# Eight 64x32 array tiles in place of four 64x64 ones, in a convolution and two-layer kernel on one Trainium2 core

## The chip, the core and the metric

The kernel runs on one core of one Trainium2 chip. The metric is the time of one execution on the device, in microseconds (us). Two executions of the kernel before took 680.85 and 681.15 us, median 681.0 us. The profile is of one further execution. In it, PE is TensorE's matmul row and PEld its weight-load row; each matmul instruction is preceded by one weight load of its own. DVE is VectorE, ACT is ScalarE, POOL is GpSimd and SP is the queue of SyncE.

## The reference

The input x has 8 sequences of 4096 tokens with 192 features. A causal convolution over 7 tokens, with one softmaxed 7-tap filter for each of 8 heads of 24 features, gives y. Then every token goes through two dense layers with a leaky ReLU between them.

```python
w = softmax(weight)                       # 8 heads x 7 taps
y[b, s, h, :] = sum_k w[h, k] * x_pad[b, s + k, h, :]
h = y @ w_in                              # 192 -> 2048
g = maximum(0.01 * h, h)
out = g @ w_out                           # 2048 -> 192, for 32768 tokens
```

The two products are 25.8 billion multiply-adds. The output has 32768 rows of 192 float32 values.

## The kernel before

The sequences are taken in pairs (index e, 0 or 1), 512 tokens of each at a time: a *block*, of which there are 32. The first two blocks are split into halves of 256 tokens, so the list `groups` has four half groups (indices 0 to 3) and 30 whole groups (indices 4 to 33). The order in which each engine gets its instructions is the order in which they are written; nothing reorders them.

**First product** (`mm1`, line 507). Features stand on partitions, 64 of sequence 0 on partitions 0 to 63 and 64 of sequence 1 on partitions 64 to 127, in three chunks c. For one u (128 of the 2048 hidden units, 16 values of u for a group), `mm1` takes the three chunks, in each the two sequences e, and in each the hidden units in slices of M: one weight load and one matmul for each. With M = 64 there are four matmuls for each c, which use four tiles of the array, 64 rows by 64 columns each: e picks the upper or lower 64 rows of the array, the slice m picks the columns and so the partitions of the output. Each sequence has its own PSUM bank. A group has 16 x 3 x 4 = 192 such matmuls, each over 512 columns (tokens). The leaky ReLU runs on ACT (line 515), from PSUM to the tile `g`, once for each u.

**Second product.** Up to and including the first whole group, `mm2_row_slot` (line 525) makes out with tokens on partitions. From the second whole group on, that is from index 5 (`i > NSW`, NSW = 4), `mm2_slot` (line 588) makes it transposed: 64 output features on partitions, for sequence 0 on the lower and sequence 1 on the upper 64, tokens as columns. One slot is one group of 128 hidden units, in two row halves rt of 64, each for both sequences e: four matmuls in four 64x64 tiles. The two row halves write to two different accumulators of the three. A group has 3 x 16 slots, so again 192 matmuls over 512 columns.

The loop at the end alternates, for each of 8 steps j: `mm1` for two u, then 5, 5, 6, 5, 5, 6, 8 and 8 slots of the second product, of the group before. Between them it issues VectorE's convolution of the next group. DVE also transposes the finished accumulators (line 610), from where they are stored.

Each matmul starts only after its weight load; the weight load of a tile's next matmul may run beside the current matmul. A matmul that has to wait for a buffer carries a semaphore wait; the others carry none. Of PE's 12442 matmuls, 672 signal a semaphore.

Near the start of the kernel the first convolution is done on PE instead (line 259): matmuls over 256 columns in 64x64 tiles with a weight load each.

The diff touches a constant, `w_out_of`, `mm2_slot` and the call of `mm1`.

Of the kernel before, what the change touches and what calls it, by code (L numbers as in the profile page):

```python
# [15 lines left out]
def kernel(  # L16
# [19 lines left out]
    CH = 64  # L36
# [15 lines left out]
    SKEW += [(1, 5), (0, 6), (1, 6)]  # L52
    CUTS = {1: (0, 6), 3: (6, 11), 5: (11, 14)}
    GB = 32
    NR = D // (2 * GB)

    const_pool = ctx.enter_context(tc.tile_pool(name="const", bufs=1))
# [177 lines left out]
    def y_of(grp, c):  # L235
        blk, t0, T = grp
        if blk not in yt:
            yt[blk] = yt_pool.tile([128, NCH, ST], BF16, name="yt")
        return yt[blk][:, c, t0 : t0 + T]
# [59 lines left out]
    for sign, off in ((1, 0), (-1, GRP - 1)):  # L299
        nc.gpsimd.affine_select(  # L300
            out=sel[:, :, 0, :], in_=sel[:, :, 0, :], compare_op=mybir.AluOpType.is_ge,
# [45 lines left out]
    w_out = const_pool.tile([128, NFC, D], BF16)  # L347
    for h in range(2):
        cs = slice(h * NFC // (2 * RUN), (h + 1) * NFC // (2 * RUN))
        nc.gpsimd.dma_start(  # L350
            out=w_out.rearrange("p (c i) d -> p c i d", i=RUN)[:, cs],
# [6 lines left out]
    def warm(n, cols=HT, to=wa[:, 0]):  # L358
# [10 lines left out]
        out=nmax, in_=w9[:, 0:K], axis=mybir.AxisListType.X,  # L369
# [3 lines left out]
        out=w9[:, 0:K], in_=w9[:, 0:K], func=mybir.ActivationFunctionType.Exp,  # L373
# [18 lines left out]
    def select(out, parts):  # L392
# [17 lines left out]
        out=taps, in_=wps_hm[..., None].to_broadcast([128, NCH, 2, K + 1, 2])  # L410
# [5 lines left out]
    def diag_wide(c, p):  # L416
# [22 lines left out]
        out=rsum, in0=wml[:, :, K:], scalar=1e-9, in1=taps[:, :, 0, K:, 0],  # L439
# [14 lines left out]
    def act_scale(out, in_, scale):  # L454
# [11 lines left out]
        out=y_of(groups[0], 0), in0=hi[:, :HT], scalar=rsum[:, 0, :], in1=low,  # L466
# [12 lines left out]
    g, po, acc2, osb, seal = {}, {}, {}, {}, None  # L479
    NSW = 2 * NHALF  # L480
# [7 lines left out]
    def mm1(grp, u, M):  # L488
        blk, t0, T = grp
        y = yt[blk]  # L490
        nf = ST // T
        ph = psum_h.tile([128, 2, ST], FP32, name="ph", tag="ph")
        chunks = range(NCH)


        wide = not (blk or t0 or u)
        order = [(i, c) for i in range(nf) for c in chunks]
        if wide:
            order = [(i, c) for c in chunks for i in range(nf)]
        for i, c in order:  # L500
            if wide and (i, c) == (0, 2):
                transpose_first(1)
            f = nf * u + i
            for e in range(2):
                ps = slice(e * CH, (e + 1) * CH)
                for m in range(0, 128, M):
                    nc.tensor.matmul(  # L507
                        out=ph[m : m + M, e, i * T : (i + 1) * T],
                        lhsT=w_in_of(f, e, c, m, m + M),
                        rhs=y[ps, c, t0 : t0 + T],  # L510
                        start=(c == chunks[0] and not (wide and i)),
                        stop=(c == chunks[-1]),
                        skip_group_check=wide,
                    )
        act = nc.scalar.activation(  # L515
            out=g[blk][:, nf * u : nf * (u + 1), :, t0 : t0 + T],
            in_=ph.rearrange("p e (i t) -> p i e t", i=nf),
            func=mybir.ActivationFunctionType.Prelu, alpha=0.01,
        )
        return act  # L520
# [41 lines left out]
            seal = evac_o(2 * p - 1)  # L562
        sync(seal, ins, "between the rounds")

    def w_out_of(ps, fc, r):
        return w_out[ps, fc, r::NR]

    def mm2_slot(q):

        nonlocal seal
        gi, fc = divmod(q, NR * NFC)
        rnd, fc = divmod(fc, NFC)
        first, last = fc == 0, fc == NFC - 1
        if first:
            for r in ((1, 0), (2,), ())[rnd]:
                acc2[gi, r] = psum_o.tile([128, ST], FP32, name="acc2", tag="po")  # L580
        for rt in range(2):
            r = (rnd + rt) % NR
            fresh = (rnd, rt) in ((0, 0), (0, 1), (1, 1))
            done = (rnd, rt) in ((1, 0), (2, 0), (2, 1))
            b, t0, T = groups[gi]
            ps = slice(rt * CH, (rt + 1) * CH)
            for e in range(2):
                ins = nc.tensor.matmul(  # L588
                    out=acc2[gi, r][e * CH : (e + 1) * CH, 0:T],
                    lhsT=w_out_of(ps, fc, r),  # L590
                    rhs=g[b][ps, fc, e, t0 : t0 + T],
                    start=first and fresh,
                    stop=last and done,
                )
                if first and not fresh:
                    sync(ins, seal, "the other row tile has left this bank")
        if last and rnd < 2:
            seal = nc.scalar.copy(out=junk, in_=junk)  # L598
            sync(seal, ins, "between the rounds")
        if last and rnd > 0:  # L600
            for r in ((), (1,), (0, 2))[rnd]:
                evac_t(gi, r)

    def evac_t(gi, r):
# [3 lines left out]
        if (gi, 0) not in osb:  # L608
            osb[gi, 0] = o_pool.tile([128, ST // GB, GB, NR], FP32, name="o_t")
        nc.vector.transpose(  # L610
            out=osb[gi, 0][:, 0 : T // GB, :, r],
            in_=acc2.pop((gi, r))[:, 0:T].rearrange("p (j k) -> p j k", k=GB),
        )
# [4 lines left out]
        for e in range(2):  # L618
            rows = out_rows[2 * rp + e, st * ST + t0 : st * ST + t0 + T, :].rearrange(
                "(j k) d -> k j d", k=GB  # L620
            )
            parts = 2 if gi == len(groups) // 2 else 1
            for h, q in product(range(2), range(parts)):
                p = (2 * e + h) * GB
                js = slice(q * T // GB // parts, (q + 1) * T // GB // parts)
                nc.sync.dma_start(
                    out=rows[:, js, h * NR * GB : (h + 1) * NR * GB],
                    in_=t[p : p + GB, js].rearrange("p j k r -> p j (k r)"),
# [41 lines left out]
    for i, grp in enumerate(groups):  # L670
        blk, t0, T = grp
        steps = T // 64
        if t0 == 0:
            g[blk] = g_pool.tile([128, NFC, 2, ST], BF16, name="g", tag="g")
        quota = plan.get(i, [16] * 4 if T == HT else [5, 5, 6, 5, 5, 6, 8, 8])

        if i == 0:
            ahead = []
        else:
            ahead = conv_jobs(groups[i + 1]) if i + 1 < len(groups) else []  # L680
        per = -(-len(ahead) // steps)
        for j in range(steps):
            early = between.get((i, j), (0, 0))
            for u in range(2 * j, 2 * j + 2):
                mm2_slots(i, early[u % 2])
                mm1(grp, u, 128 if i <= NSW else CH)
                if i == 0 and u == 0:
                    evac_first(1, nc.vector.tensor_copy, nc.vector.tensor_copy)
                    spread_up(0, slice(2, 3), far)
                    conv_1 = conv_jobs(groups[1], (1,))  # L690
                    run([conv_1[:3]])
                    spread_down(1)
                    spread_up(1, slice(0, 1), near)
                    spread_up(1, slice(2, 3))
                    run([conv_1[3:5]])
                    spread_up(1, slice(0, 1), far)
                    run([conv_1[5:]])
                    pe_0, evac_0 = pe_conv_jobs(groups[1], 0)
                    pe_2, evac_2 = pe_conv_jobs(groups[1], 2, cross=True)
                if i == 0 and u in CUTS:  # L700
                    cut = slice(*CUTS[u])
                    run(pe_0[cut], pe_2[cut])
                if i == 0 and u == 5:
                    evac_0(nc.vector.tensor_scalar_mul)
                    evac_2(nc.vector.tensor_scalar_mul, nc.vector.tensor_scalar_mul)
                if i == 0 and u == 6:
                    transpose_first(2)
                    evac_first(2, nc.vector.tensor_copy, nc.vector.tensor_copy)
            jobs = ahead[per * j : per * (j + 1)]
            if T == ST:  # L710


                jobs = ahead[len(ahead) * j // steps : len(ahead) * (j + 1) // steps]
                for job in jobs:
                    job()
                jobs = []
            mm2_slots(i, quota[j] - sum(early))
            if i == 1 and j == 1:
                load_x(3, transpose_x(2))
            for job in jobs:  # L720
                job()
            if i == 0 and j == 3:
                transpose_half(3)

            last_half = t0 + T == ST
            if i == NSW and j == steps - 1:
                evac_o(LAST - 1)
                slot = NSW * NR * NFC
            if j == steps // 4 and last_half and blk > 0:
                load_x(blk + 3)  # L730
            if j == steps // 2 and last_half and blk > 0:
                transpose_x(blk + 2)
# [35 lines left out]
```

## Time and profile before

| | |
|---|---|
| time, median of 2 runs | 681.0 us (680.85 to 681.15) |
| span of the profiled execution | 679.2 us |
| PE busy | 674.9 us, 12442 matmuls |
| PEld busy | 446.3 us, 12442 weight loads |
| DVE busy | 481.2 us |
| ACT busy | 517.6 us |
| granted TensorE clock | 1.000 throughout |
| DMA | 53.27 MB, of them 1.59 MB instructions in 97 packets |

The span is the time from the first to the last instruction in one execution. It leaves 1.8 us of the 681.0 us outside. The busy time of PE counts overlapping matmuls once; the mean duration of one matmul (376 ns for 512 columns) is longer than its share of the time, as several run at once. A line number is that of the listing above.

### The profile page before, as it was taken

To read this page: it belongs to the slowest core of one execution; us is meant where nothing else is said; L and a number is where in the kernel's file an instruction comes from. 1 tells how busy PE (TensorE), PEld (TensorE's weight loads), DVE (VectorE), ACT (ScalarE), POOL (GpSimd) and SP (SyncE) were. 2 spreads that over 40 slices of the span, in tenths; PEclk is the share of its full clock that TensorE was granted. 3 is DMA by queue.
4 is the path that set the end of the run, shared out by engine and by line. 5 is a ranking of instruction groups with operands and counts; after the bars stand their busy time and mean duration, and the time that the engine had idled before them with its cause. 6 is when DMAs were issued, how large, how long until landed. Compare 5 with 4: busy or idle time off the path is not lost.

```text
span 679.2 us, 27092 instructions
## 1 busy us (share of the span) xinstructions
PE 674.9 (99%) x12442; PEld 446.3 (66%) x12442; DVE 481.2 (71%) x816; ACT 517.6 (76%) x601; POOL 147.4 (22%) x208
## 2 busy tenths in 40 slices
PE   9999999999999999999999999999999999999998
PEld 6997666666666666666666666666666666666667
DVE  7989477866768766778667687667786676876612
ACT  7899877777787777777777777778777777777781
POOL 8455221122211222211222112222022220000000
PEclk9999999999999999999999999999999999999999
DMA  9999755655737656556556566567365573321123
GB/s 149 99 119 104 52 85 83 84 64 67 96 74 93 76 54 86 84 85 86 66 63 92 80 92 78 56 83 94 73 87 69 60 96 71 72 56 33 34 49 94
DMA packets 213970, 53.27 MB, mean 78 GB/s; under 512 B 209312, under 2 KB 213536, under 8 KB 213856
## 3 DMA queue, kind: packets, MB, share of 16 engines
q0 software_dynamic: 98832, 13.97, 30.3%
q1 hardware_dynamic: 115008, 37.57, 28.0%
q8 instruction: 97, 1.59, 0.9%
q14 instruction: 17, 0.14, 0.1%
q10 hardware_dynamic: 16, 0.00, 0.0%
HBM read 28.31 MB, written 25.17 MB: 79 GB/s over the span
## 4 chain that ended last, share of the span: by engine, by line
PE 98%; DVE 1%; ACT 0%; issue 0%; ACTq 0%
PE ph L507 49%; PE acc L588 44%; PE po L525 5%; PE acc L259 0%; DVE diag L420 0%; PE ptr L167 0%; ACT L366 0%; ACTq L288 0%; DVE w_in L322 0%; DVE yt L465 0%; DVE o_sb L638 0%; DVE x_half L155 0%; ACT w L372 0%; DVE w_in L326 0%; ACT junk L366 0%
## 5 line engine op out<-in xcount | busy, mean ns | idle before, releaser
L515 ACT ACTIVATE g<-ph 128x1024 bf16<-128x1024 f32 x512 | 496.6, 1021 | 139.8 <-PE ph L507 139.6
L228 DVE SCALAR_TENSOR_TENSOR yt<-xt,wk,yt 128x512 bf16<-128x512 bf16 (+1 forms) x582 | 380.1, 715 | 0.2
L507 PE MATMUL ph<-yt,w_in 64*64 64x512 bf16 (+2 forms) x6048 | 377.5, 369 | 0.3 <-DVE yt L465 0.3
L588 PE MATMUL acc<-g,w_out 64*64 64x512 bf16 x5568 | 339.9, 376 | 0.0
L507 PEld LDWEIGHTS <-w_in 64*64 64x64 bf16 (+1 forms) x6048 | 229.7, 131 | 103.4 <-issue 1.1
L588 PEld LDWEIGHTS <-w_out 64*64 64x64 bf16 x5568 | 178.2, 118 | 118.8
L96 POOL DMA_DIRECT2D x_bf<-in_x_dram x180 | 133.9, 774 | 407.6 <-DMA xt<-x_bf 405.6
L610 DVE STREAM_TRANSPOSE o_t<-acc 128x512 f32<-128x512 f32 x87 | 72.9, 875 | 182.2 <-PE acc L588 182.2
L525 PE MATMUL po<-w_out,g 64*128 64x192 bf16 (+1 forms) x640 | 36.8, 243 | 0.0
L525 PEld LDWEIGHTS <-g 64*128 64x128 bf16 (+1 forms) x640 | 32.6, 95 | 3.2 <-issue 0.4
L222 DVE TENSOR_SCALAR yt<-xt,wk 128x512 bf16<-128x512 bf16 (+1 forms) x97 | 28.8, 320 | 2.4 <-DMA xt<-x_bf 2.4
L598 ACT COPY junk<-junk 128x1 f32<-128x1 f32 x58 | 11.1, 191 | 4.1
L638 DVE COPY o_sb<-po 128x192 f32<-128x192 f32 x8 | 2.8, 356 | 6.8 <-PE po L525 3.9
L638 ACT COPY o_sb<-po 128x192 f32<-128x192 f32 x16 | 5.1, 323 | 0.3
L259 PE MATMUL acc<-xt,diag 64*64 64x256 bf16 x126 | 4.7, 272 | 0.1
L149 POOL DMA_DIRECT2D x_half<-in_x_dram x6 | 4.3, 732 | 0.9 <-DMA w_in<-in_moe_w_in_dram 0.9
L259 PEld LDWEIGHTS <-diag 64*64 64x64 bf16 x140 | 3.7, 106 | 1.0 <-issue 0.4
L360 PE MATMUL warm<-const-bfloat16-1.0 128*128 128x512 bf16 (+2 forms) x8 | 3.3, 577 | 0.8 <-PEq L752 0.8
L145 POOL DMA_DIRECT2D x_rows<-in_x_dram x4 | 2.9, 746 | 0.0
L316 POOL DMA_DIRECT2D w_in<-in_moe_w_in_dram x5 | 2.9, 593 | 0.0
L360 PEld LDWEIGHTS <-const-bfloat16-1.0 128*128 128x128 bf16 x10 | 1.2, 128 | 2.2 <-issue 2.2
L326 DVE COPY w_in<-w_in 64x512 bf16<-64x512 bf16 (+1 forms) x7 | 2.3, 337 | 0.2
(52 smaller groups left out, 25.9 us busy)
## 6 DMA issues: line engine op xcount, KB each, us to landing
out_dram<-o_t SPq DMA_DIRECT2D x112, 192.0 KB, 4.7
x_bf<-in_x_dram POOLq DMA_DIRECT2D x180, 64.0 KB, 3.1
out_dram<-o_sb SPq DMA_DIRECT2D x8, 192.0 KB, 2.8
xt<-x_bf SPq DMA_TRANSPOSE x90, 3.2
w_out<-in_moe_w_out_dram POOLq DMA_DIRECT2D x2, 384.0 KB, 8.3
out_dram<-o_t SPq DMA_DIRECT2D x8, 96.0 KB, 2.4
out_dram<-o_sb SPq DMA_DIRECT2D x8, 96.0 KB, 1.7
w_in<-in_moe_w_in_dram POOLq DMA_DIRECT2D x2, 256.0 KB, 5.5
```

Source lines behind the costliest of these rows:

```text
L96: ins = nc.gpsimd.dma_start(out=t[:, c, :, e, :], in_=src[2 * rp + e, :, :, c * CH : (c + 1) * CH],)
L222: lambda s=src, d=dst, c=c: nc.vector.tensor_scalar_mul(d, s, wk[:, c, 0:1])
L228: lambda s=src, d=dst, c=c, k=k: nc.vector.scalar_tensor_tensor(out=d, in0=s, scalar=wk[:, c, k : k + 1], in1=d, op0=mybir.AluOpType.mult, ...
L259: lambda k=k, p=p, a=a, ps=ps, to=to, acc=accs[e]: nc.tensor.matmul(out=acc[to, :T], lhsT=diag[c][ps, p, k, :], rhs=xt[0][ps, c, a : a + T ...
L360: nc.tensor.matmul(out=to[:, 0:cols], lhsT=ones[:, 0:128], rhs=ones[:, 0:cols], start=True, stop=True,)
L507: nc.tensor.matmul(out=ph[m : m + M, e, i * T : (i + 1) * T], lhsT=w_in_of(f, e, c, m, m + M), rhs=y[ps, c, t0 : t0 + T], start=(c == chun ...
L515: act = nc.scalar.activation(out=g[blk][:, nf * u : nf * (u + 1), :, t0 : t0 + T], in_=ph.rearrange("p e (i t) -> p i e t", i=nf), func=my ...
L525: return nc.tensor.matmul(out=po[m], lhsT=g[b][ps, fc, e, s * 128 : (s + 1) * 128], rhs=w_out[ps, fc, :], start=start, stop=stop,)
L588: ins = nc.tensor.matmul(out=acc2[gi, r][e * CH : (e + 1) * CH, 0:T], lhsT=w_out_of(ps, fc, r), rhs=g[b][ps, fc, e, t0 : t0 + T], start=fi ...
L598: seal = nc.scalar.copy(out=junk, in_=junk)
L610: nc.vector.transpose(out=osb[gi, 0][:, 0 : T // GB, :, r], in_=acc2.pop((gi, r))[:, 0:T].rearrange("p (j k) -> p j k", k=GB),)
L638: ins = copy(out=o_sb[:, n % 2, :], in_=po.pop(n))
```

## The change

From group 5 on, both products are cut into slices of 32 output partitions in place of 64. In the first product M goes from 64 to 32, so that for each chunk and sequence there are four weight loads of 64x32 and four matmuls in place of two. In the second product each of the four matmuls of a slot becomes two, each with 32 of the 64 output features. Weights are picked with the same strides as before, 32 columns at a time. The tiles of the array are 64 rows by 32 columns, eight of them. What each element of the output adds up, the order of u and slots, the waits, ACT's and DVE's work and the DMAs of data stay as they are.

```diff
     GB = 32
+    CT = 32
     NR = D // (2 * GB)
 ...
-    def w_out_of(ps, fc, r):
-        return w_out[ps, fc, r::NR]
+    def w_out_of(ps, fc, r, m):
+        return w_out[ps, fc, r + m * NR : (m + CT) * NR : NR]
 ...
-            for e in range(2):
+            for e, m in product(range(2), range(0, CH, CT)):
                 ins = nc.tensor.matmul(
-                    out=acc2[gi, r][e * CH : (e + 1) * CH, 0:T],
-                    lhsT=w_out_of(ps, fc, r),
+                    out=acc2[gi, r][e * CH + m : e * CH + m + CT, 0:T],
+                    lhsT=w_out_of(ps, fc, r, m),
                     rhs=g[b][ps, fc, e, t0 : t0 + T],
 ...
-                mm1(grp, u, 128 if i <= NSW else CH)
+                mm1(grp, u, 128 if i <= NSW else CT)
```

## The prediction

> **What bounds the kernel now.** I read the page first: busy times, then the chain of work that ended last.
>
> ```profile
> span 679.2 us, 27092 instructions
> PE 674.9 (99%) x12442; PEld 446.3 (66%) x12442; DVE 481.2 (71%) x816; ACT 517.6 (76%) x601; POOL 147.4 (22%) x208
> ...
> PE 98%; DVE 1%; ACT 0%; issue 0%; ACTq 0%
> ```
>
> PE is busy in 99% of the span and carries 98% of the chain. A busy PE need not be at its peak, so next come the stretches of one group and the chain's pieces inside a group.
>
> ```profile
> core 0: us, PE busy (x) PEld busy (x) DVE busy (x) ACT busy (x) POOL busy (x), PEclk, DMA share, GB/s
> 301.00:321.72 20.72, 20.72 (x388) 13.18 (x384) 15.04 (x26) 15.89 (x19) 4.46 (x6) 1.00 0.61 80
> 321.72:342.44 20.72, 20.72 (x388) 13.19 (x384) 15.03 (x25) 15.89 (x19) 4.45 (x6) 1.00 0.60 77
> ```
>
> ```profile
> 100.04 1.29 PE ph L507 x24
> 101.34 1.73 PE acc L588 x32
> 103.06 1.29 PE ph L507 x24
> ```
>
> One whole group takes 20.72 us and has 384 matmuls (the x388 counts four that began earlier). Four run at once, one in each 64x64 tile: 96 *sets* of four, 215.8 ns each. The pieces agree: 24 matmuls, six sets, in 1.29 us. The trace's single records show how a set goes: its four matmuls start within 10 ns, the next four 216 ns later, and the weight loads of the next set start about 2 ns after the matmuls of this one, so they are hidden. ACT needs 15.89 and DVE 15.04 of the 20.72 us; neither holds PE up in a set. The 29 groups that the change touches are 29 x 20.72 = 600.9 us of the span, or 2784 sets.
>
> How much of 215.8 ns is streaming? The same tiles with 256 columns (line 259, near the start) come in sets of 108.6 ns (from 6.054 to 7.481 us in the records, 13.1 sets). So 256 columns more cost 107.2 ns, 512 columns 214.4 ns, and 1.4 ns of a set are fixed.
>
> **The change part by part.**
>
> *Streaming.* Each 64x32 matmul still streams 512 columns, and does half the work. Eight at once, in eight tiles, are one set of today: 214.4 ns at least. The most that can be gained is the 1.4 ns, 2784 x 1.4 = 3.9 us. Whether eight streams run at the full rate no row shows, since the rows have at most four tiles at once. Bounds: full rate (0 us) or, if the two halves of today's column tile take turns, each set twice, +600.9 us. I take full rate: today's two column tiles already stream from the same partitions side by side (in the second product even different data, the two sequences) without losing time to each other, and that is the nearest row.
>
> *Instructions.* Added are 29 x 384 = 11136 matmuls and as many weight loads. A set becomes eight pairs of load and matmul, to be delivered in 215.8 ns, that is 27.0 ns a pair, or 13.5 ns an instruction. Today's stage asks for 54 ns a pair. The nearest rows that ask for more are those of line 259:
>
> ```profile
> L259 PE MATMUL acc<-xt,diag 64*64 64x256 bf16 x126 | 4.7, 272 | 0.1
> ```
>
> ```profile
> 5.26 2.22 PEld L259 LDWEIGHTS <-diag 64*64 64x64 bf16 x82
> ...
> 12.33 0.74 PE L259 MATMUL acc<-xt,diag 64*64 64x256 bf16 x20
> ```
>
> 82 loads in 2.22 us: less the last one's 0.107 us, 81 steps of 26.1 ns. The steadiest part of it runs at 108.6/4 = 27.2 ns a pair, and there the array sets the pace, not the delivery. 8 x 27.2 = 217.4 ns for a set, +1.6 ns, 2784 x 1.6 = +4.5 us at most if that pace were the limit. But some of the 82 pairs may have stood decoded in front of PE. Two waits of PE's sequencer bound this:
>
> ```profile
> L259 PEldq EVENT_SEMAPHORE  x1: 51/51/51, 5.4 to 5.4; - x1
> ...
> L181 PEldq EVENT_SEMAPHORE  x1: 51/51/51, 4.4 to 4.4; - x1
> ```
>
> In the built program 67 instructions lie from the first to the second; the records have them at 4.358 and 5.387 us, and what the second waits for had come at 4.38. So the sequencer took at most 1.029/67 = 15.4 ns an instruction, and possibly much less, as it may have stood behind a full queue. Nor can it be much worse later: from the second wait's end (5.438) to the last load of this stretch (7.377) it delivered 110 more, at most 17.6 ns each. With 15.4 ns a set of 16 instructions takes 246 ns, +30.6 ns, 2784 x 30.6 = +85 us. So delivery costs between 0 and +85 us. I take +2.5 us, half of the 4.5: the pace of line 259 is the row nearest to what is asked.
>
> A rule of the Trainium skill speaks against this. "Runtime: NRT & Kernel Launch", section "Instruction fetch mechanics", gives an issue floor of about 20 cycles an instruction; with the sequencer clock of 1.2 GHz that "TensorE: Matmul & The Clock Gate", Part 1, states, an estimate is 16.7 ns, 267 ns a set, +142 us, 823 us in all. The 15.4 ns above is a little under that floor, and no run here shows a steady stream that would test it.
>
> *Weight loads.* Today 64 columns a load, then 32. The load row of a set today is hidden with room: a load's record lasts 118 (line 588) to 133 ns (line 507) of 215.8, four at a time, starting 3 to 4 ns apart. Eight loads start within some 28 ns by the same spacing and end before the set does. This holds if loads are pulled ahead of seven waiting matmuls; the rows show three. If a part of the loads came only after the matmuls ahead of them, a load's latency would be bare in each set: between 28 ns (load at 6.026, its matmul at 6.054) and 107 ns (the record's length at 256 columns): +78 to +298 us. I take nothing, because the loads of today's four tiles all go ahead at once.
>
> *Instruction fetch.* The page has
>
> ```profile
> q8 instruction: 97, 1.59, 0.9%
> ```
>
> 0.9% of 16 engines' 679.2 us over 97 packets is 1.0 us each, for 16.4 KB, some 256 instructions (24884 on PE over 97). A packet lasts 6.9 us of work today, 3.45 us then. In the records a fetch begins up to 2.4 us ahead of PE's reaching that place, but about 0 us in the third of fetches that fall beside the output stores, so those are some 2.2 us late, and 1.0 us goes on the transfer: 3.2 us of 3.45. Lowest cost 0; if one fetch in a group is 1 us late, 29 x 1 = +29 us. I take +0.5 us: PE's queue covers part of a microsecond.
>
> *Waits.* The semaphore waits stand at the same places of the work. The first matmul of a second u is released by ACT at 111.106 us in one case and needed at 111.311, 205 ns to spare; the loads behind that wait went at 111.149. Eight need 28 ns to issue and 133 ns to land, 111.310, and just fit: a cost of 0, at the worst some 30 ns for 8 such places in 29 groups, 7 us. The DMA of data, ACT and DVE are unchanged and have 4.8 us or more of slack in each group.
>
> Sum: the profiled execution has 679.2 us span and 1.8 us around it, which is the 681.0 us median. 681.0 + 0 (streams) + 2.5 (delivery) + 0 (loads) + 0.5 (fetch) + 0 (waits) = **684.0 us**, no change that counts.
>
> **The rivals.**
>
> 1. *Delivery becomes the bound* (ends slower): PE's sequencer cannot keep 13.5 ns an instruction over a whole group. Its place is every set of the 29 groups. Its price is 16 x (d - 13.5) ns a set for d ns an instruction; it decides over 2% from d = 13.8. At the bound of 15.4: 766 us. For it: nothing in the trace asks for such a pace for longer than 2.2 us, and there is no idle time in which to catch up. Against it: 82 pairs at 26.1 ns.
> 2. *Loads not ahead, or streams that take turns.* Price +78 to +298 us (759 to 979 us) for loads, up to 1282 us for streams. For it: eight tiles at once appear nowhere in the trace. Against it: nothing is lost today with two column tiles and three matmuls passed.
> 3. *Late instruction fetches*, 695 to 740 us, at 1 to 2 us for each group. For it: the budget halves. Against it: the mean fetch is short, and the queue is ahead of PE.
> 4. *Faster.* The fixed 1.4 ns vanish: 677 us. Even then not by 2%. That the change does not do what it says is rival 2's last case: 64x32 tiles that do not run together.
>
> **How the numbers follow.** Forecast (677 to 694 us) 0.45; rival 1: 0.22; rival 2: 0.20; rival 3: 0.12; any gain over 2%: 0.01. The likeliest single case gives the time. The range takes in the gain's end (677), rivals 3 and 1 and the start of rival 2: 677 to 800 us; left out is rival 2 beyond 800, some 0.15, and little below. Two per cent is about what a measurement of this kernel can tell from no change: faster 0.01, same 0.45, slower 0.54.
>
> **What would show it.** In the changed kernel's profile a group should again take 20.7 us, with 768 matmuls, and pieces of 48 matmuls on line 507 in 1.29 us. In the records eight matmuls should start within some 30 ns and the next eight 216 ns after the first. If delivery is the bound, matmuls come one by one at 30 ns a pair with no set to be seen, and the load row starts just ahead of each. If loads are late, each set has a group that starts at once and a few that lag by 28 to 107 ns. If the streams take turns, the starts fall in two groups 214 ns apart. If fetches are late, there are gaps of about 1 us, one for every 256 instructions, beside q8 packets. I am wrong above all if a stream of PE instructions has a limit that a 2 us stretch cannot show.

## The result and the profile after

The changed kernel takes 765.6 us (median of 2 runs, 764.35 to 766.89) against 681.0 us: 1.124 times as long, 95% interval 1.120 to 1.129. It is slower by 84.6 us. The profiled execution has a span of 762.6 us.

The page of the changed kernel, its busy times and the chain of work that ended last:

```profile
span 762.6 us, 49364 instructions
PE 704.3 (92%) x23578; PEld 483.9 (63%) x23578; DVE 484.8 (64%) x816; ACT 519.8 (68%) x601; POOL 147.2 (19%) x208
...
q8 instruction: 184, 3.01, 1.7%
...
PE 65%; DVE 28%; issue 5%; DMA 1%; POOL 1%; DVEq 0%; POOLq 0%
```

PE is now idle for 8% of the span, and the instruction queue q8 carries 184 packets where it carried 97. DVE, ACT and POOL are busy for within 1% of their times before, and the granted clock is 1.00 as it was. The chain puts 28% on DVE; what that is worth is seen below. The pieces of the chain inside one group show where the time goes. The columns are start (us), length (us) and what:

```profile
100.79 0.07 issue
100.86 1.49 PE ph L508 x44
102.35 1.29 PE acc L589 x48
103.64 0.88 PE ph L508 x36
104.52 0.34 issue
104.86 0.63 PE ph L508 x12
105.49 1.73 PE acc L589 x64
107.22 1.29 PE ph L508 x48
108.51 0.01 PE acc L589 x4
108.53 0.61 issue
```

Where PE works, it works at the old pace: 48 matmuls of half the size take 1.29 us, as 24 did, so six sets of eight at 215 ns. In the single records eight matmuls start within some 50 ns (median of the sets) and the next eight 216 ns after the first. Between two pieces marked "issue", in which PE waits for nothing that the profile shows, lie 128 matmuls (12 + 64 + 48 + 4 from 104.86 to 108.53 us). With their loads these are 256 instructions.

The records point to the cause. In the stage there are 133 gaps of more than 225 ns between two matmuls' starts. Of these, 132 end 1.24 to 1.57 us (5% to 95%; median 1.41) after the end of a packet of q8; the other one is the change of the tile shape at the stage's end. The 132 also keep to one count: with the kernel's matmuls numbered from 0, each gap falls just before a matmul 94 + 128k (1374, 1502, 1630 and so on), in whichever of the two products. A group has 768 matmuls, six times 128, so the count alone could still be six places in a group; the run halves_5of6 below, with 704 a group, decides. A *block* stands below for such a stretch of 256 instructions, not for a block of tokens. Taking 190 ns off each gap for the usual step between sets, the 132 hold 78.7 us, nearly all of the 84.6. The views by engine name other releasers for some:

```profile
PEld L589 <- issue: 51.6, 64, 1.8
PEld L508 <- issue: 47.9, 75, 1.2
PE acc L589 <- DVE yt L229: 22.2, 22, 1.5
PE ph L508 <- issue: 21.9, 46, 0.9
PE acc L589 <- issue: 6.4, 16, 0.6
```

These are the waits, with us in total, times and the longest. The 22 waits "on DVE" are of the same gaps: each ends 1.2 to 1.6 us after a fetch. The chain's 28% of DVE starts from such inferred releasers; the places of these gaps do not bear it out, nor does halves_first below, where DVE has the same work and PE does not wait.

**The cycle of a fetch.** In the changed kernel's records PE starts again on a new block; the next q8 packet starts 1.2 us later (median; 1.06 to 2.4 from 5% to 95%), takes 1.10 us (mean), and 1.4 us after its end PE has the block after. That makes 3.7 us. The first part is often longer, 1.43 us in the mean, and with it the sum is the 3.94 us that lie on average between one packet's start and the next. A block of 256 instructions at 13.5 ns each lasts 3.45 us. In the kernel before, a block lasted 6.9 us and no gap stands behind a fetch.

A word on the spacing of packets, which returns below: since one packet goes with each block, it is the stage's time divided by its blocks, in a kernel that waits for fetches and in one that doesn't. By itself it shows nothing. What tells the two apart is whether there are gaps, where they stand and when they end.

### The profile page after: what moved, and what is told of

It reads as the page before. It is cut to its first block, busy times and chain, and to the rows that moved or that the text cites. A ratio compares the mean times of both kernels' runs of the same rounds, so it can differ in the third digit from the quotient of the medians.

```text
span 762.6 us, 49364 instructions
## 1 busy us (share of the span) xinstructions
PE 704.3 (92%) x23578; PEld 483.9 (63%) x23578; DVE 484.8 (64%) x816; ACT 519.8 (68%) x601; POOL 147.2 (19%) x208
## 4 chain that ended last, share of the span: by engine, by line
PE 65%; DVE 28%; issue 5%; DMA 1%; POOL 1%; DVEq 0%; POOLq 0%
PE acc L589 31%; PE ph L508 30%; DVE yt L229 21%; DVE o_t L611 5%; PE po L526 4%; DVE yt L223 2%; DMA w_in<-in_moe_w_in_dram 1%; POOL w_in L317 0%; POOL x_rows L146 0%; DVE w_in L327 0%; POOL sel L301 0%; PE ptr L168 0%; PE acc L260 0%; DVE w_in L323 0%; DVE o_sb L639 0%
## 5 line engine op out<-in xcount | busy, mean ns | idle before, releaser
L508 PE MATMUL ph<-yt,w_in 64*32 64x512 bf16 (+1 forms) x11616 | 439.9, 374 | 23.8 <-issue 21.9
L589 PE MATMUL acc<-g,w_out 64*32 64x512 bf16 x11136 | 399.2, 377 | 30.7 <-DVE yt L229 22.2
L508 PEld LDWEIGHTS <-w_in 64*32 64x32 bf16 (+1 forms) x11616 | 262.9, 104 | 129.5 <-issue 47.9
L589 PEld LDWEIGHTS <-w_out 64*32 64x32 bf16 x11136 | 225.8, 97 | 139.6 <-issue 51.6
L611 DVE STREAM_TRANSPOSE o_t<-acc 128x512 f32<-128x512 f32 x87 | 76.8, 937 | 260.6 <-PE acc L589 260.6
L223 DVE TENSOR_SCALAR yt<-xt,wk 128x512 bf16<-128x512 bf16 (+1 forms) x97 | 32.2, 377 | 3.4 <-PE ph L508 3.3
```

Source lines behind the costliest of these rows:

```text
L223: lambda s=src, d=dst, c=c: nc.vector.tensor_scalar_mul(d, s, wk[:, c, 0:1])
L508: nc.tensor.matmul(out=ph[m : m + M, e, i * T : (i + 1) * T], lhsT=w_in_of(f, e, c, m, m + M), rhs=y[ps, c, t0 : t0 + T], start=(c == chun ...
L589: ins = nc.tensor.matmul(out=acc2[gi, r][e * CH + m : e * CH + m + CT, 0:T], lhsT=w_out_of(ps, fc, r, m), rhs=g[b][ps, fc, e, t0 : t0 + T] ...
L611: nc.vector.transpose(out=osb[gi, 0][:, 0 : T // GB, :, r], in_=acc2.pop((gi, r))[:, 0:T].rearrange("p (j k) -> p j k", k=GB),)
```

## Experiments

Three theories were held against each other. **F**: the fetch of instructions, one block of 256 at a time, sets the pace. **D**: PE's sequencer needs 15.4 ns for each instruction (rival 1 of the prediction). **T**: eight tiles cost time by themselves.

### As many instructions without 64x32 tiles: halves_both

```diff
-            for e in range(2):
+            P = 2 if T == ST and M == CH else 1
+            W = T // P
+            for h, e in product(range(P), range(2)):
 ...
-                        out=ph[m : m + M, e, i * T : (i + 1) * T],
+                        out=ph[m : m + M, e, i * T + h * W : i * T + (h + 1) * W],
-                        rhs=y[ps, c, t0 : t0 + T],
+                        rhs=y[ps, c, t0 + h * W : t0 + (h + 1) * W],
```

From group 5 on P is 2 and W is 256. The base is the kernel before, and the second product is cut in the same way.

> The kernel before, with its 64x64 tiles, but from group 5 on each matmul over 512 columns is cut into two over 256, in both products: as many matmuls and weight loads as in the changed kernel (768 of each for a group), and no 64x32 tile. Theory F (instruction fetch: a block of 256 instructions arrives only about every 3.95 us, and 256 instructions at 13.5 ns last 3.45 us): a group has six blocks, 23.7 us in place of 20.72, so 29 x 2.9 = +84 us and about 4 us more for the fixed 1.4 ns of each set: 760 to 775 us, with PE idle about once in 256 instructions, each time until 1.2 to 1.6 us after the end of a fetch. Theory D (PE's sequencer needs 15.4 ns for each instruction): the same total, but no bursts and gaps. Theory T (eight tiles cost some 30 ns a set by themselves): 683 to 689 us.

Measured: 767.2 us, 1.126 times the kernel before (1.124 to 1.128). Its q8 has 184 packets, 3.94 us apart on average in the stage. Its 126 gaps of more than 150 ns all stand at the same place of a block as in the changed kernel and end 1.25 to 1.58 us (5% to 95%) after a packet. T falls: the same loss comes without one 64x32 tile. F and D stand.

### Half the added instructions: halves_first

The same cut in the first product alone.

> The kernel before, with only the first product's matmuls cut into two over 256 columns from group 5 on: 576 matmuls, 1152 instructions and 4.5 blocks for a group. Theory F: 20.72/4.5 = 4.6 us of work for a block, above the 3.95 us of a fetch, so nearly nothing is lost: 682 to 690 us. A cost in proportion to the added instructions (half of the 84 us): 721 to 727 us. Theory D: also nearly nothing, since 1152 x 15.4 ns = 17.7 us is under 20.72. Theory T: 682 to 685 us.

Measured: 685.3 us, 1.0058 times (1.0041 to 1.0075). Half of the added instructions cost 4 us, not 42. It has 140 fetches, in the stage 4.63 us apart. No gap of over 225 ns is left but one, where the tile shape changes at the stage's end; the uncut second product has its usual steps of about 206 ns between the last matmul of a set of four and the next. The loss has a threshold, as F and D both say. Some 2 us of the 4 are the fixed 1.4 ns for 1392 more sets; the rest was not resolved.

### Just below the threshold: halves_5of6

```diff
+            P = 2 if r < 2 else 1     # accumulators 0 and 1 in halves, 2 whole
```

> 64x64 tiles, the first product's matmuls all cut into two over 256 columns and the second product's in two of its three accumulators: 704 matmuls, 1408 instructions, 5.5 blocks of 256 for a group. 20.72/5.5 = 3.77 us of work for a block, just under the mean fetch of 3.94 us in the changed kernel. Theory F: a fetch that takes its mean or longer is felt, a short one not: 5.5 x 3.94 = 21.7 us a group, some 29 us more, 695 to 725 us. In proportion to the added instructions (320 of 384): 681 + 70 = 751 us. Theory D (15.4 ns an instruction, 21.7 us a group): 709 us.

Measured: 714.9 us, 1.050 times (1.048 to 1.052): inside F's range and far from the 751 us of a cost in proportion. D's 709 us is near it too. The three points with 4.5, 5.5 and 6 blocks for a group give +4, +34 and +86 us. The work of a block lasts 4.6, 3.77 and 3.45 us in them, against the 3.94 us of a mean fetch in the changed kernel. The 39 gaps of over 225 ns, of 158 blocks, all end behind a fetch and hold some 25 of the 34 us (beyond a mean step of 27 ns). They all fall before a matmul 94 + 128k again, though a group now has five and a half times 128: the count is that of the instruction stream and not a place in the group's work. That fits F: with 3.77 us of work it is the longer fetches that are felt. Where the other 9 us go was not resolved; by 1.4 ns a set, the 80 added sets of each group would make 3 of them.

### Fetch without work to hide it: tiles32_halves_first

The changed kernel with the first product's matmuls also cut into halves.

> The changed kernel, with the first product's 64x32 matmuls also cut into two over 256 columns: 1152 matmuls, 2304 instructions, nine blocks for a group. The array's work asks for 2.3 us a block, so this measures the fetch by itself. Theory F: 9 x 3.95 = 35.6 us a group, 681 + 29 x 14.9 = 1112 us (1050 to 1150, as quiet fetches may come faster), with PE idle for over a third of the time. Theory D: 2304 x 15.4 ns = 35.5 us, the same total. Theory T (30 ns a set, 144 sets): 800 to 815 us.

Measured: 1084.7 us, 1.593 times (1.587 to 1.598), inside F's range. The fetches are 3.84 us apart, and 29 groups x (9 x 3.84 - 20.72) = +401 us on 681 gives 1082; this only books the spacing back into time. More telling is that the parts of the fetch are those of the changed kernel (1.34, 1.10 and 1.40 us), though the work of a block is a third shorter. Its chain inside a group, in the same columns as before:

```profile
305.75 1.81 PE acc L591 x57
307.56 0.98 PE ph L510 x67
308.53 0.68 issue
309.22 0.63 PE ph L510 x28
309.85 1.08 PE acc L591 x40
310.93 0.78 PE ph L510 x60
311.70 1.26 issue
```

Again 128 matmuls (28 + 40 + 60) lie between two stretches of "issue". They take 2.49 us, and these 256 instructions come straight after a wait: 9.7 ns an instruction. In the piece before the first "issue", 67 matmuls with their loads take 0.98 us, 7.3 ns an instruction, in a stretch of 134 instructions. D's 15.4 ns would need 3.94 us for the block. D falls as a rate of single instructions; as an average over a block it is the same as F, 3.94 us / 256 = 15.4 ns.

### Fewer transfers beside the fetch

Does the fetch share the queues with the kernel's data? Three runs leave data movement out and change nothing on PE. First the stores:

```diff
             for h, q in product(range(2), range(parts)):
+                if gi < len(groups) - 2:
+                    continue
```

> The changed kernel without the stores of the second product's transposed output, but for the last two groups (the output rows of the others are left unwritten; all arithmetic is done). In the changed kernel's trace the gap of PE is 0.61 us on average behind a fetch beside stores or transposes (80 of 171), 0.48 us beside the loads of x (36) and 0.21 us behind a quiet one (55). Theory F with contention: the fetches beside stores become like the quiet ones, 80 x 0.4 = 32 us less: 725 to 745 us. Theory F without contention, theory D and theory T: 760 to 766 us, as nothing on PE changes.

Measured: 764.3 us, 1.122 times (1.118 to 1.126): no gain, against what F with contention expected. The stretches show why. This is the changed kernel, the columns being PE, PEld, DVE, ACT and POOL busy with counts, clock, DMA share and GB/s:

```profile
70.00:140.00 70.00, 65.10 (x2308) 43.26 (x2303) 42.16 (x68) 47.53 (x54) 13.36 (x18) 1.00 0.57 66
440.00:500.00 60.00, 54.96 (x1955) 36.30 (x1944) 40.25 (x66) 39.84 (x45) 8.91 (x12) 1.00 0.57 73
```

And this the run without stores:

```profile
70.00:140.00 70.00, 53.50 (x1724) 33.20 (x1717) 32.62 (x52) 36.07 (x41) 48.98 (x66) 0.93 1.97 126
440.00:500.00 60.00, 59.00 (x2113) 40.43 (x2105) 41.75 (x68) 44.59 (x51) 0.00 (x0) 1.00 0.02 5
```

POOL now issues the loads of x in bursts (up to 140 us, then from 180 to 240 and from 360 to 400), with 126 GB/s in the stretch up to 140 us; the likely reason, not tested by itself, is that the transposes no longer stand behind stores in SP's queue, so that the loads' buffers come free early. There fetches are 5.6 to 7.1 us apart (the ones that start at 103.4, 110.6 and 116.1 us), PE's gaps grow to 2.0 to 2.6 us, and even the granted clock goes to 0.93. PE does 24.6 matmuls per us in place of 33.0. Where next to nothing moves (5 GB/s), it does 35.2 in place of 32.6. One edit made a quiet part and a crowded one, and the total says nothing. So the next run takes the loads away:

```diff
     def load_x(blk, after=None):
-        if blk >= NBLK:
+        if blk >= NB:
             return
 ...
         if st == 0:
             new_xt(rp)
+        if rp:
+            return
 ...
     def new_xt(rp):
+        if rp:
+            xt[rp] = xt[0]
+            return
```

> The changed kernel, but x is loaded and transposed for the first pair of sequences alone; the other three pairs repeat its convolution and products, so their output rows are those of the first pair. All work on PE, ACT and DVE and all stores remain. Theory F with contention: in the run without stores PE took 28.4 ns a matmul where neither loads nor stores ran, 30.9 in the changed kernel on average. With the loads gone from some 26 of 29 groups and the stores left: between 713 and 750 us. Theory F without contention, and theory D: 760 to 766 us.

Measured: 739.5 us, 1.086 times (1.084 to 1.088), inside F's range with contention: 26 us less, with fetches 3.78 us apart. And without either:

> The run before this one, also without the stores of the second product's transposed output but for the last two groups. Theory F with contention: after the first pair's blocks a fetch has the queues to itself: 28.4 x 768 ns = 21.8 us a group, 1.1 us above 20.72, so 681 + 29 x 1.1 = 713 us, and some more for the first groups: 708 to 725 us. What is left over 681 is the fetch itself, 3.7 us against 3.45 of work. Theory F without contention, and theory D: 760 to 766 us.

Measured: 721.3 us, 1.059 times (1.057 to 1.061), another 18 us less, with fetches 3.69 us apart. Its stretches in the stage:

```profile
100.00:200.00 100.00, 98.09 (x3519) 70.87 (x3504) 68.33 (x109) 72.34 (x82) 0.00 (x0) 1.00 0.02 5
300.00:400.00 100.00, 96.26 (x3432) 63.97 (x3420) 67.17 (x107) 70.44 (x81) 0.00 (x0) 1.00 0.02 4
500.00:600.00 100.00, 98.06 (x3520) 67.00 (x3512) 68.10 (x108) 72.22 (x83) 0.00 (x0) 1.00 0.02 5
```

PE does 34.3 to 35.2 matmuls per us with next to no data moving. PE has the same instructions in all of these runs, so a rate of its sequencer cannot explain the 44 us between 765.6 and 721.3; a fetch that shares the DMA can. The records show which part of the fetch it is. From PE's entering a block to the packet's start it takes 1.43 us on average in the changed kernel, 1.28 us without loads and 1.19 us without loads and stores, and 3.0 us in the crowded stretch without stores (blocks from 80 to 135 us). The transfer takes 1.10 to 1.15 us in all four, and from its end to PE's next matmul it is 1.39 to 1.40 us in three and 1.58 us in the crowded stretch. So other traffic makes the fetch mostly start late; it hardly makes it slower. Over 174 blocks the differences of 0.15 and 0.09 us make 26 and 16 us, against 26 and 18 us measured.

In this order of leaving out, the 84.6 us come apart into 26 us for the loads and transposes beside the fetch, 18 us for the stores, and 40 us that a fetch costs with the DMA nearly to itself. The stores' 18 us are not what they cost alone: with the loads in place, leaving them out gained nothing that counts (764.3 us).

### 64x32 tiles in one product alone: tiles32_first

```diff
-                mm1(grp, u, 128 if i <= NSW else CH)
+                mm1(grp, u, 128 if i <= NSW else GB)
```

> The kernel before, with 64x32 tiles in the first product alone: 4.5 blocks for a group, 4.6 us each. PE now goes over from 64x32 to 64x64 tiles and back 16 times a group; in the kernel before, a change of tile shape shows as 260 and 308 ns between sets in place of 216. Theory F: no loss to fetches, only the 16 changes: 29 x 16 x (44 to 92 ns) = 20 to 43 us: 701 to 724 us, with the gaps at the changes and not at fetches. Theory T (30 ns for each of 48 sets a group), with the changes: 743 to 766 us.

Measured: 745.8 us, 1.095 times (1.093 to 1.097). The total lies in the range of T and above that of F; taken alone it would have misled. The pieces of its chain say otherwise:

```profile
300.14 1.43 PE ph L507 x48
301.57 1.44 PE acc L588 x24
303.01 1.43 PE ph L507 x48
304.44 1.22 PE acc L588 x20
```

There is no "issue" here, and fetches are 5.1 us apart. Each stretch, in either tile shape, is 0.14 us longer than in the kernel before (1.43 and 1.44 in place of 1.29, 1.22 in place of 1.08). With 16 stretches in each of 29 groups that is 65 us, which is the whole loss. Inside a stretch the records still have sets of eight, and of four, 216 ns apart. So a change of shape costs 0.14 us, where 44 to 92 ns had been read from two single changes between other shapes, and the tiles themselves cost nothing that could be seen.

## Why the prediction was right or wrong

The time is inside the range of 677 to 800 us, and slower by over 2% had 0.54. But the case that gave the number, 684.0 us and no change that counts, is not what happened. That the range holds 765.6 us is luck in good part: it reaches so far for rival 1, whose mechanism did not occur, and for the start of rival 2; rival 3, whose mechanism did, ended at 740 us.

*Streaming: right.* Eight tiles run at once at the full rate, 216 ns a set.

*Weight loads: right.* The eight loads of the next set start within some 2 ns of this set's matmuls, and sets stay 216 ns apart; rival 2, both halves of it, did not occur.

*Delivery: the step as it was taken was right, rival 1 right in its sum alone.* Within a block 13.5 ns an instruction is no limit, nor is 9.7 over a whole block or 7.3 over 134 instructions, and no run shows the 2.5 us that were added for delivery. The bound of 15.4 ns, read from two waits near the start, and the 766 us from it agree with the result by chance: the fetch averages 3.94 us over 256 instructions, which is also 15.4. A number that agrees is no proof of its mechanism; that the gaps end behind fetches, and the runs without loads and stores, decide. The floor of about 20 cycles that the Trainium skill gives ("Runtime: NRT & Kernel Launch", "Instruction fetch mechanics") is not one for PE's loads and matmuls here: the 9.7 ns over a whole block are under 12 cycles of the 1.2 GHz that "TensorE: Matmul & The Clock Gate", Part 1, states for the sequencer. Nor is crossing a block always "mostly hidden", as the section on instruction fetch says: with 6.9 us of work to a block it was, but with 3.45 us it costs 0.49 us on average (84.6 us over 174 blocks).

*Instruction fetch: the step that failed.* The prediction put "3.2 us of 3.45" for a fetch and took +0.5 us. Its terms were a late start of up to 2.2 us, read relative to the earliest fetch, and 1.0 us of transfer. It had no term for the 1.4 us from a packet's end to PE's next instruction, and none for the 1.2 us from PE's entering a block to even an early packet's start. Neither could be read in the kernel before: a block lasts 6.9 us there, no gap stands behind a fetch, and packets start between 1.0 us before and 1.7 us after PE reaches a block. With them a quiet fetch takes 3.7 us and the mean one 3.94, over the 3.45 of the work, so not one fetch in a group is late but most of the six. Rival 3 had the mechanism and its place, but was priced at 1 to 2 us for a group, 695 to 740 us. Measured are 2.9 us for a group (84.6/29). What the 1.2 and the 1.4 us consist of, no run shows.

*Waits, ACT, DVE: right.* None of them holds up a set; DVE's share in the chain is a label for fetch gaps.

*The sentence on what would show it* named the picture that came: gaps, one for every 256 instructions, beside q8 packets.

## What to carry to other kernels

A PE instruction stream has a budget that no engine's busy time shows: in this kernel some 3.7 to 4 us for each 256 instructions, 128 pairs of load and matmul, and more beside heavy DMA. Count instructions against it before cutting matmuls smaller: with pairs closer than about 31 ns (3.94 us over 128) the fetch, not the array, set the pace here, while half as many added instructions cost 4 us. When PE idles at "issue" or on a releaser that makes no sense, compare the ends of the gaps with the instruction queue's packets, and count whether the gaps stand a fixed number of instructions apart.

## What the runs showed of the hardware that was not expected

- After a packet of instructions has landed, PE's next matmul starts 1.4 us later, in every run with fetch gaps (5% to 95%: 1.23 to 1.61 us).
- The kernel's own DMA lengthens a fetch: 3.69 us from one to the next with little data moving, 3.94 beside loads and stores at about 70 GB/s, 5.6 to 7.1 us at 126 GB/s. Nearly all of it is a later start (1.19, 1.43 and 3.0 us after PE enters a block); the transfer stays at 1.10 to 1.15 us. Leaving stores out gained nothing, and the loads of x bunched up in that run.
- A change between 64x32 and 64x64 tiles costs 0.14 us for each stretch (65 us in 464 changes).
